# The first chunk of a scan with buffers of its own, a wider spread of its decays, and a first gate in halves, in a fused scan and feed-forward kernel

## The chip, the cores and the metric

The kernel runs on one core of a Trainium2 chip. The metric is the device time of one execution in microseconds (us). The engines are PE (matrix products), DVE (vector), ACT (scalar), POOL (GpSimd) and SP, which issues the DMAs.

## The reference

A chunked state-space scan over 4 batches, 8 heads and 768 positions (head width 32, state width 16) is followed by a gated feed-forward layer over the 3072 tokens (model width 256, hidden width 1536). All is fp32.

```python
# scan, chunk by chunk, for each batch and head
cum = np.cumsum(log(clip(a, 1e-6, 1)), axis=-1)
L = exp(cum[..., :, None] - cum[..., None, :]) * causal
y_intra = ((C @ B.T) * L) @ x
y_inter = (C @ state) * exp(cum)[..., None]
y = y_intra + y_inter
state = exp(sum(la)) * state + sum_j(B_j x_j exp(cum[-1] - cum_j))
# feed-forward over the tokens
gate = 1 / (1 + exp(-(x @ w_gate)))
out = (gate * (x @ w_val)) @ w_out
```

## The kernel before

The 768 positions are cut into six chunks of 128. A chunk has four units, one for each batch b. A unit transposes B and C (`pt`, copied to `bct` by ACT), multiplies them (`pcb`), builds decays (`ab`, a scan on DVE), multiplies products and decays (`m`, DVE) and adds decayed B (a second part of `m`, "bdec", on POOL in the first chunk), multiplies with x (`py`, `mm`) and carries a state (`st`, `sb`). The result y goes to SBUF as `xh` (from the second chunk on in two parts, `xh` and `xl`), one quarter of its columns from each unit.

The first chunk is treated apart (`FirstUnit`). It works on two halves of 64 positions, so a unit has two results: `py` and `mm`. The state between the halves goes through `tr`, a transpose on DVE, to four more matmuls into `mm` (line 642), with `cd`, which is C times decays (`pc`, `pp`). In its `spread`, PE copies decays of 32 rows (b, head) to all partitions: sixteen matmuls of 32x64 into `pa`, which DVE then scans to `ab`. `bct` and `m` have two buffers each, `pcb` has one. The transposed and copied halves of y are read in two steps: `early` for the first, the end of `result` for the second.

After a chunk's scan its feed-forward tokens follow: 12 gates `pg` and 12 values `pv` (f = 0 to 11), the product `h`, and four projections `po` over three blocks of four f each. In the first chunk weights are whole fp32 values (`wr`, prepared in "split" steps on ACT, DVE and POOL, lines 308 to 323) and a gate takes four PE instructions; later ones use two fp32r parts `w` (prepared in "part" steps on ACT and POOL, lines 334 and 336) and six matmuls. From the second chunk on POOL also makes the low part of `h` (line 736).

No scheduler of the compiler orders this: `run()` takes tasks, each with a due time (`DUES` or a formula of constants), and emits their steps in the order of a small plan of engine times. So one table sets the order on every engine. PSUM has three `mm` buffers (pt, pa, pc, mm, pg, pv, po), four banks for `pcb` and one for `py`. A matmul writes a buffer only when its readers are done with it.

Of the kernel before, what the change touches and what calls it, by code (L numbers as in the profile page):

```python
# [17 lines left out]
DUES = {  # L18
# [8 lines left out]
}  # L27
WARM = 3
# [12 lines left out]
GV0 = 1.75  # L41
GV0_T = 3.3
PART = 48.0
PROJ_T = 4.2
P0 = 37.3
UNIT0 = 3.4
CONV_D = 3.0
CONV = -23.4
UNIT1 = 61.1
UNIT1_D = 6.4  # L50
FFN1 = 107.3
UNIT_T = 3.4
UNIT_D = 0.0
AHEAD = 21.9
STATE = 14.7
SPARE = 4.0
# [7 lines left out]
def tile_ssd_then_gated_ffn(  # L64
# [68 lines left out]

    of_b = const.tile([NB * H, NB], F32, name="of_b")
    eye_bh = eye[: NB * H, : NB * H]
    nc.vector.tensor_reduce(of_b, eye_bh.rearrange("p (b h) -> p b h", b=NB), axis=mybir.AxisListType.X, op=ALU.add)
    head = const.tile([NB * H, H], F32, name="head")
    nc.vector.tensor_reduce(head, eye_bh.rearrange("p (b h) -> p h b", b=NB), axis=mybir.AxisListType.X, op=ALU.add)
    of_row = hp.tile([NB * H, P], F32, tag="h4", name="of_row")
# [212 lines left out]
    class Unit:  # L352
# [15 lines left out]
        def products(self):  # L368

            c, b, u = self.c, self.b, self.u  # L370
            needs = [("bc", u), ("bct", u - 1 if c > 1 else -1), ("cb", u - 2), ("cd", u - 2)] + ([("x", 0, NB - 1)] if c == 1 else [])
# [5 lines left out]
            yield step("act", 0.9 if c else 1.1, [("cb", u - 2), ("cd", u - 2)], [("bct", u)], banks=-1)  # L377
            self.bct = wk.tile([P, 4, L], F32, tag="bct", name=f"bct{self.nm}")
            if c:
                nc.scalar.copy(self.bct[:, :2].rearrange("p k l -> p (k l)"), pt[:, : 2 * L])  # L380
            else:
                nc.scalar.copy(self.bct[:, 0], pt[:, :L])
            for g in range(NG):
                nc.scalar.mul(self.bct[:, 2 + g], pt[:, L : 2 * L], of_g[:, g : g + 1])
            if c == 0:
                nc.scalar.copy(self.bct[:, 1, L2:], pt[:, L + L2 : 2 * L])
            units[u] = self
            if u <= NB:
                yield step("pe", 0.85 if c else 0.47, [], [("cb", u)], cb=1)
                self.multiply()  # L390
# [158 lines left out]
    class FirstUnit(Unit):  # L549
# [11 lines left out]
        def spread(self):  # L561

            b, u = self.b, self.u
            yield step("pe", 1.15, [("a0",)], banks=1)
            pa = ps_mm.tile([P, 512], F32, tag="mm", name=f"pa{b}")
            for k in range(H):
                h = b * H + k
                for i in range(2):
                    rows = slice(32 * i, 32 * i + 32)
                    one = eye[rows, 32 * i + h : 32 * i + h + 1].broadcast_to([32, L2])  # L570
                    nc.tensor.matmul(
                        pa[i * L2 : (i + 1) * L2, k * L2 : (k + 1) * L2], one, ac[rows, i * L2 : (i + 1) * L2],
                        start=True, stop=True,
                    )
            yield step("dve", 1.22, [], [("scan", u)], banks=-1)
# [6 lines left out]
        def multiply(self):  # L582
            self.pcb = ps_cb.tile([P, NQ, 512], F32, tag="pcb", name=f"pcb{self.nm}")
            for q in range(NQ):
                qs = slice(32 * q, 32 * q + 32)
                for i in range(2):
                    half = slice(i * L2, (i + 1) * L2)
                    nc.tensor.matmul(
                        self.pcb[half, q, : NG * L2], self.bct[qs, 0, half], self.bct[qs, 2:4, half],
                        start=True, stop=True,  # L590
                    )
# [21 lines left out]
        def result(self):  # L613
            u, b = self.u, self.b
            yield step("dve", 0.68, [("cb", u), ("scan", u), ("ph", u - 2)], [("mult", u)], cb=-1)
            nc.vector.tensor_tensor(
                out=self.second()[:, :, :L2].rearrange("p (q g) l -> p q g l", g=NG),
                in0=self.pcb[:, :, : NG * L2].rearrange("p q (g l) -> p q g l", g=NG),
                in1=self.dec.rearrange("p (q g) l -> p q g l", g=NG), op=ALU.mult,
# [88 lines left out]
    def gate(k, f):  # L708
        yield step("pe", GV_T / 2 if k else GV0, needs_of(k, f, 0), [("pg", k, f)] + used(k, f, 0), banks=1)
        pm = products_of(k, f, 0)  # L710
        yield step("act", ACT_MM, [], [("sig", k, f)], banks=-1, g=1)
        gs[k, f] = wk.tile([P, 512], F32, tag="g", name=f"g{k}_{f}", bufs=3)
        nc.scalar.activation(gs[k, f], pm, AF.Sigmoid)  # L713

    def value(k, f):
        makes = [("pv", k, f)] + ([("gv", k)] if f == NF - 1 else [])
        yield step("pe", GV_T / 2 if k else GV0, needs_of(k, f, 1) + [("pg", k, f)], makes + used(k, f, 1), banks=1)
        pm = products_of(k, f, 1)
        if k == 0:
# [21 lines left out]
    def needs_of(k, f, j):  # L741
        return [("w" if k else "whole", f // 2 * 2 + j)] + [("x", k, i) for i in range(NB)] + ([("pv", k, f - 1)] if f else [])

    def products_of(k, f, j):
# [87 lines left out]
    nc.vector.tensor_scalar(out=ac, in0=a0, scalar1=1e-6, scalar2=1.0, op0=ALU.max, op1=ALU.min)  # L832
    nc.vector.memset(ac.rearrange("p (s l) -> p s l", l=L2)[:, :, :1], 0.0)
    chunks = "p (c l) -> p c l"

# [152 lines left out]
```

## Time and profile before

| | |
|---|---|
| runs | 387.51, 387.96, 388.02 us, median 387.96 |
| profiled execution | 387.17 us, span 384.7 us, mean granted PE clock 0.972 |
| DVE, ACT, POOL busy | 203.0, 149.8, 166.6 us |
| moved by DMA | 31.39 MB, mean 82 GB/s |

A group's line gives source line, engine, operation, tiles (output and inputs), count, then busy time, mean ns and the idle time before it with what ended it. A timeline row gives start, length, engine, line, output and inputs, count and, in brackets, the idle time before it and its releaser. Two groups of the first chunk's feed-forward and two of POOL's:

```profile
L323 POOL TENSOR_TENSOR wr<-wr 128x512 int32<-128x512 int32 x18 | 21.8, 1218 | 35.6 <-ACT wr L321 31.3
L336 POOL TENSOR_TENSOR w<-wr,w 128x512 fp32r<-128x512 f32 x18 | 27.6, 1532 | 4.5 <-ACT w L334 4.4
```

### The profile page before, as it was taken

How to read it: one execution, taken by the hardware profiler on the slowest of the kernel's cores; microseconds unless marked ns; L12 is line 12 of the kernel's file. 1: busy time of each engine (PE TensorE's matmuls, PEld its weight loads, DVE VectorE, ACT ScalarE, POOL GpSimd, SP SyncE). 2: the span in 40 equal slices, each digit the busy share in tenths (PEclk: the TensorE clock that was granted, in tenths of full speed). 3: DMA queues.
4: the chain of work that ended last, by engine and by line, in shares of the span. 5: the costliest groups of instructions: out<-in, count | busy, mean ns of one | idle time of the engine just before them, and what ended most of it. 6: DMA issues, size and time to landing. Idle time of an engine off the chain costs nothing.

```text
span 384.7 us, 6190 instructions
## 1 busy us (share of the span) xinstructions
PE 375.2 (98%) x2368; PEld 287.8 (75%) x2368; DVE 203.0 (53%) x311; ACT 149.8 (39%) x319; POOL 166.6 (43%) x136
## 2 busy tenths in 40 slices
PE   8689999999999999999999999999999999999996
PEld 4444444677788888877888877888877888888885
DVE  4676779977893566457870157970155220122201
ACT  3364564533465521254340254340254340235310
POOL 2353345465889950334770034780032340044410
PEclk9658999999999999999999999999999999999999
DMA  7899793075530087138600038600000000000000
GB/s 87 237 369 386 102 212 88 1 146 129 84 108 2 10 123 185 41 42 152 157 9 27 27 36 158 159 8 29 27 9 0 2 0 29 27 0 2 0 24 32
DMA packets 107462, 31.39 MB, mean 82 GB/s; under 512 B 76554, under 2 KB 102730, under 8 KB 107434
## 3 DMA queue, kind: packets, MB, share of 16 engines
q1 hardware_dynamic: 107434, 31.01, 35.0%
q8 instruction: 19, 0.31, 0.3%
q14 instruction: 9, 0.07, 0.1%
HBM read 27.66 MB, written 3.34 MB: 81 GB/s over the span
## 4 chain that ended last, share of the span: by engine, by line
PE 93%; SPq 3%; DMA 1%; DVE 1%; issue 1%; POOL 0%; ACT 0%
PE pv L760 22%; PE pg L760 21%; PE po L793 14%; PE po L794 7%; PE pg L751 6%; PE po L783 6%; PE pv L751 5%; PE pcb L489 3%; PE py L527 2%; PE py L519 2%; SPq L253 1%; SPq L267 1%; DMA wr<-in_moe_w_val_dram 1%; PE pt L375 1%; PE po L790 1%; PE py L446 1%
## 5 line engine op out<-in xcount | busy, mean ns | idle before, releaser
L736 POOL TENSOR_TENSOR h<-g,h 128x512 fp32r<-128x512 f32 x60 | 92.1, 1537 | 129.7 <-ACT h L734 129.6
L760 PE MATMUL pg<-xh,w 128*128 128x512 f32 x240 | 85.4, 396 | 0.0
L760 PE MATMUL pv<-xh,w 128*128 128x512 f32 x240 | 84.6, 393 | 0.0
L793 PE MATMUL po<-w,h 128*128 128x512 f32 x228 | 81.0, 399 | 0.0
L730 DVE TENSOR_TENSOR g<-pv,g 128x512 f32<-128x512 f32 x60 | 41.2, 686 | 67.7 <-PE pv L760 59.3
L794 PE MATMUL po<-w,h 128*128 128x256 f32 x228 | 64.0, 281 | 0.0
L734 ACT CAST h<-g 128x512 fp32r<-128x512 f32 x60 | 37.2, 620 | 65.0 <-DVE g L730 64.7
L713 ACT ACTIVATE g<-pg 128x512 f32<-128x512 f32 x72 | 43.0, 597 | 45.9 <-PE pg L760 25.9
L760 PEld LDWEIGHTS pv<-xh,w 128*128 128x128 f32 x240 | 45.0, 188 | 10.7 <-issue 1.4
L760 PEld LDWEIGHTS pg<-xh,w 128*128 128x128 f32 x240 | 45.1, 188 | 10.0 <-ACT xh L538 0.3
L793 PEld LDWEIGHTS po<-w,h 128*128 128x128 f32 x228 | 42.8, 188 | 10.8 <-issue 0.2
L401 DVE TENSOR_TENSOR_SCAN ab<-ab,delta 128x1024 f32<-128x1024 f32 x20 | 49.2, 2461 | 2.5 <-DMA ab<-a_z 2.5
L760 PE MATMUL pg<-xl,w 128*128 128x512 f32 x120 | 46.8, 390 | 0.0
L760 PE MATMUL pv<-xl,w 128*128 128x512 f32 x120 | 46.8, 390 | 0.0
L794 PEld LDWEIGHTS po<-w,h 128*128 128x128 f32 x228 | 43.1, 189 | 0.3
L808 DVE TENSOR_TENSOR o<-po,o 128x256 f32<-128x256 f32 x20 | 8.5, 424 | 63.8 <-ACT o L806 63.8
L323 POOL TENSOR_TENSOR wr<-wr 128x512 int32<-128x512 int32 x18 | 21.8, 1218 | 35.6 <-ACT wr L321 31.3
L806 ACT COPY o<-po 128x256 f32<-128x256 f32 x20 | 7.4, 372 | 69.6 <-PE po L794 69.1
L336 POOL TENSOR_TENSOR w<-wr,w 128x512 fp32r<-128x512 f32 x18 | 27.6, 1532 | 4.5 <-ACT w L334 4.4
L477 POOL TENSOR_TENSOR sb<-st,of_h 128x256 f32<-128x256 f32 x20 | 18.7, 940 | 20.9 <-DVE st L469 17.5
L760 PEld LDWEIGHTS pv<-xl,w 128*128 128x128 f32 x120 | 22.5, 188 | 4.5
L760 PEld LDWEIGHTS pg<-xl,w 128*128 128x128 f32 x120 | 22.6, 188 | 4.1
(105 smaller groups left out, 436.4 us busy)
## 6 DMA issues: line engine op xcount, KB each, us to landing
ab<-a_z SPq DMA_DIRECT2D x20, 512.0 KB
wr<-in_moe_w_gate_dram SPq DMA_DIRECT2D x6, 512.0 KB
wr<-in_moe_w_val_dram SPq DMA_DIRECT2D x6, 512.0 KB
wr<-in_moe_w_out_dram SPq DMA_DIRECT2D x6, 512.0 KB
out_dram<-o SPq DMA_DIRECT2D x24, 128.0 KB
xn<-in_x_dram SPq DMA_DIRECT2D x10, 256.0 KB
bn<-in_B_dram SPq DMA_DIRECT2D x40, 32.0 KB
cn<-in_C_dram SPq DMA_DIRECT2D x40, 32.0 KB
```

The costliest lines, as they stand in the source:

```text
L323: nc.gpsimd.tensor_tensor(out=lw.bitcast(I32), in0=hw.bitcast(I32), in1=lw.bitcast(I32), op=ALU.add)
L336: engines[eng].tensor_tensor(out=lo, in0=lw, in1=hi.bitcast(F32), op=ALU.subtract)
L401: nc.vector.tensor_tensor_scan(out=t.rearrange("p h l -> p (h l)"), data0=t.rearrange("p h l -> p (h l)"), data1=delta.rearrange("p h l -> ...
L713: nc.scalar.activation(gs[k, f], pm, AF.Sigmoid)
L730: nc.vector.tensor_tensor(out=g, in0=pm, in1=g, op=ALU.mult)
L734: copies[eng](hh, g)
L736: engines[eng].tensor_tensor(out=hl, in0=g, in1=hh.bitcast(F32), op=ALU.subtract)
L751: nc.tensor.matmul(pm, whole[f // 2 * 2 + j][:, kt, fs], xb[0][0][:, kt], start=(kt == 0), stop=(kt == NK - 1))
L760: nc.tensor.matmul(pm, w[:, part, kt, fs], xx[:, kt], start=(i == 0), stop=(i == 3 * NK - 1))
L783: nc.tensor.matmul(acc[:, :DM], hs[k, f][:, js], whole[NF + f // 2][:, f % 2], start=(f == 0), stop=(f == NF - 1))
L793: nc.tensor.matmul(acc, hh, w.rearrange("p i m -> p (i m)"), start=(f == 0), stop=False, skip_group_check=True)
L794: nc.tensor.matmul(acc[:, :DM], hl, w[:, 0, :], start=False, stop=(f == NF - 1), skip_group_check=True)
```

## The change

Four things are changed.

1. The spread uses two matmuls a unit, over 32 rows and 512 columns each. Their input `apart` (the decays times a table of heads) is made once, half by DVE and half by POOL; `of_b` and `head` become tables of 64 rows.
2. In the first chunk `bct` lies in buffers of its own for all four units, taken from tiles that `h` uses later, and the four products `pcb` lie in one PSUM tile, made as soon as `bct` is there.
3. The first gate and the first value are computed in halves of 256 columns: the first halves need x of batches 0 and 1 only.
4. `DUES` and the constants beside it are others, so the order moves on every engine.

```diff
 DUES = {
-    "spread0": 133, "products0_0": -376, "result0_0": -282, "before1_0": -70, "products1_0": 182, "decays1_0": 10,
+    "p": 51.5, "before0_0": 75.7, "state0_0": 85.1, "x1_0": 142.5, "before1_0": -134.0, "decays1_0": -57.3,
...
-GV0_T = 3.3
-PART = 48.0
+GV0_T = 3.4
+PART = 41.9
...
-P0 = 37.3
-UNIT0 = 3.4
-CONV_D = 3.0
-CONV = -23.4
-UNIT1 = 61.1
-UNIT1_D = 6.4
-FFN1 = 107.3
-UNIT_T = 3.4
+P0 = 35.5
+UNIT0 = 4.5
+CONV_D = 6.3
+CONV = -30.0
+UNIT1 = 60.6
+UNIT1_D = 8.2
+FFN1 = 85.9
+UNIT_T = 14.9
...
-AHEAD = 21.9
-STATE = 14.7
+AHEAD = 46.7
+STATE = 30.0
...
-        free = {"sp": 1.0, "pe": 1.2 + 1.7 * WARM, "act": 3.5, "dve": 4.8, "pool": 4.2, "none": 0.0}
+        free = {"sp": 1.0, "pe": 1.2 + 1.7 * WARM, "act": 3.5, "dve": 6.0, "pool": 6.2, "none": 0.0}
...
-            self.bct = wk.tile([P, 4, L], F32, tag="bct", name=f"bct{self.nm}")
+            if c:
+                self.bct = wk.tile([P, 4, L], F32, tag="bct", name=f"bct{self.nm}")
+            else:
+
+                if ("bct", b // 2) not in got:
+                    got["bct", b // 2] = hp.tile([P, 2, 4, L], F32, tag=f"h{b // 2}", name=f"bct{self.nm}")
+                self.bct = got["bct", b // 2][:, b % 2]
...
-            if u <= NB:
-                yield step("pe", 0.85 if c else 0.47, [], [("cb", u)], cb=1)
+            if c == 0:
+                yield step("pe", 0.47, [], [("cb", u)])
+                self.multiply()
+            elif u == NB:
+                yield step("pe", 0.85, [("mult", v) for v in range(NB)], [("cb", u)], cb=1)
                 self.multiply()
...
-            for k in range(H):
-                h = b * H + k
-                for i in range(2):
-                    rows = slice(32 * i, 32 * i + 32)
-                    one = eye[rows, 32 * i + h : 32 * i + h + 1].broadcast_to([32, L2])
-                    nc.tensor.matmul(
-                        pa[i * L2 : (i + 1) * L2, k * L2 : (k + 1) * L2], one, ac[rows, i * L2 : (i + 1) * L2],
-                        start=True, stop=True,
-                    )
+            for i in range(2):
+                rows = slice(32 * i, 32 * i + 32)
+                nc.tensor.matmul(
+                    pa[i * L2 : (i + 1) * L2], of_b2[rows, b : b + 1].broadcast_to([32, L2]),
+                    apart[rows].rearrange("p h l -> p (h l)"), start=True, stop=True,
+                )
...
-            self.pcb = ps_cb.tile([P, NQ, 512], F32, tag="pcb", name=f"pcb{self.nm}")
+
+            if "pcb" not in got:
+                got["pcb"] = ps_cb.tile([P, NQ, NB, NG * L2], F32, tag="pcb", name="pcb0")
+            self.pcb = got["pcb"][:, :, self.b]
...
+        if (k, f) == (0, 0):
+
+            yield step("pe", GV0 / 2, [("whole", 0), ("x", 0, 0), ("x", 0, 1)], [("pg half",)], banks=1)
+            pm = first_half(0)
+            yield step("pe", GV0 / 2, [("x", 0, 2), ("x", 0, 3)], [("pg", k, f)])
+            second_half(0, pm)
...
+    def half_of(j, pm, columns):
+        for kt in range(NK):
+            nc.tensor.matmul(
+                pm[:, columns], whole[j][:, kt, :P], xb[0][0][:, kt, columns], start=(kt == 0), stop=(kt == NK - 1)
+            )
...
+    apart = hp.tile([R2, H, L2], F32, tag="h2", name="apart")
+    for i, engine in ((0, nc.vector), (1, nc.gpsimd)):
+        rows = slice(32 * i, 32 * i + 32)
+        engine.tensor_tensor(
+            out=apart[rows], in0=ac[rows, i * L2 : (i + 1) * L2].rearrange("p (o l) -> p o l", o=1).broadcast_to([32, H, L2]),
+            in1=head2[rows].rearrange("p (h o) -> p h o", o=1).broadcast_to([32, H, L2]), op=ALU.mult,
+        )
```

On PE, the end of the first chunk's scan before the first gate. A row is a line, an operation, the output and inputs with their numbers, and a shape; the first number behind a name is the unit's or the f's. Before:

```order
L642 MATMUL mm_1_379<-cd_1_334,tr_1_406 32x2x64 x4
L630 MATMUL py_2_429<-m_2_332,xn_1_144 32x80
L598 MATMUL pc_3_456<-bct_3_367,perm 128x64
L630 MATMUL py_3_466<-m_3_447,xn_1_144 32x80
L642 MATMUL mm_2_430<-cd_2_421,tr_2_459 32x2x64 x4
L642 MATMUL mm_3_467<-cd_3_461,tr_3_493 32x2x64 x4
L751 MATMUL pg_0_509<-xh_353,wr_148 128x512 x2
L751 MATMUL pv_0_532<-xh_353,wr_199 128x512 x2
```

In the changed kernel the same place reads (the rows of py alternate with rows of mm in both; one of each group is shown):

```order
L647 MATMUL py_2_366<-m_2_297,xn_1_145 32x80
L659 MATMUL mm_1_327<-cd_1_283,tr_1_355 32x2x64 x4
L615 MATMUL pc_3_394<-bct_2_217,perm 128x64
L659 MATMUL mm_2_367<-cd_2_359,tr_2_399 32x2x64 x4
L647 MATMUL py_3_417<-m_3_353,xn_1_145 32x80
L784 MATMUL pg_0_442<-xh_309,wr_147 128x256 x2
L659 MATMUL mm_3_418<-cd_3_402,tr_3_446 32x2x64 x4
L784 MATMUL pv_0_458<-xh_309,wr_173 128x256 x2
```

The third unit's mm stands ahead of the fourth unit's py, and the fourth unit's mm stands between the first half of the gate and that of the value.

On DVE, the first chunk's products and transposes in the changed kernel, from the fourth decay scan on (`wt` and `wr` are the weight split):

```order
L633 TENSOR_TENSOR m_2_297<-pcb_175,ab_2_212 128x8x64
L655 STREAM_TRANSPOSE tr_0_295<-mm_0_265 128x32
L633 TENSOR_TENSOR m_1_222<-pcb_175,ab_1_200 128x8x64
L315 TENSOR_SCALAR wt_313<-wt_313 128x512
L679 SCALAR_TENSOR_TENSOR st_110<-tr_0_295,pp_184 128x32
L317 TENSOR_SCALAR wt_313<-wt_313 128x512
L633 TENSOR_TENSOR m_3_353<-pcb_175,ab_3_227 128x8x64
L655 STREAM_TRANSPOSE tr_1_355<-py_1_326 128x32
L618 TENSOR_TENSOR cd_2_359<-pc_2_322,pp_184 128x128
L655 STREAM_TRANSPOSE tr_1_355<-mm_1_327 128x32
L315 TENSOR_SCALAR wt_350<-wt_350 128x512
L322 SCALAR_TENSOR_TENSOR wr_173<-wr_173,wt_313 128x512
```

The third unit's product goes ahead of the second's, and operations of the weight split lie between the second unit's transposes and the third's.

On POOL, the end of chunk 1's gates before (`w` are weight parts, `h` the low parts of h, `sb` the state's matrix for the scan):

```order
L736 TENSOR_TENSOR h_9_1335<-g_9_1321,h_9_1335 128x512
L336 TENSOR_TENSOR w_1358<-wr_512,w_1358 128x2x256
L736 TENSOR_TENSOR h_10_1384<-g_10_1345,h_10_1384 128x512
L477 TENSOR_TENSOR sb_114<-st_110,of_h 128x256
L477 TENSOR_TENSOR sb_115<-st_111,of_h 128x256
L736 TENSOR_TENSOR h_11_1467<-g_11_1439,h_11_1467 128x512
```

And in the changed kernel:

```order
L341 TENSOR_TENSOR w_1305<-wr_439,w_1305 128x2x256
L494 TENSOR_TENSOR sb_116<-st_112,of_h 128x256
L341 TENSOR_TENSOR w_1355<-wr_455,w_1355 128x2x256
L766 TENSOR_TENSOR h_10_1371<-g_10_1339,h_10_1371 128x512
L494 TENSOR_TENSOR sb_114<-st_110,of_h 128x256
L766 TENSOR_TENSOR h_11_1412<-g_11_1367,h_11_1412 128x512
L494 TENSOR_TENSOR sb_115<-st_111,of_h 128x256
L341 TENSOR_TENSOR w_1385<-wr_474,w_1385 128x2x256
```

The last weight part stands behind the last h of the chunk, and ten parts instead of eight come between the first h and the last operation that this projection needs.

More of the change, by code (lines that the diff above doesn't have):

```diff
@@ L132, in tile_ssd_then_gated_ffn @@
     nc.gpsimd.tensor_copy(delta2, eye2.rearrange("p (o l) -> p o l", o=1).broadcast_to([P, H, L2]))
[L134 to L138, printed above, removed]
+    R2 = 2 * NB * H
+    of_b2 = const.tile([R2, NB], F32, name="of_b")
+    eye_bh = eye[:R2, :R2]
+    nc.vector.tensor_reduce(
+        of_b2, eye_bh.rearrange("p (o b h) -> p b o h", o=2, b=NB), axis=mybir.AxisListType.XY, op=ALU.add
+    )
+    head2 = const.tile([R2, H], F32, name="head")
+    nc.vector.tensor_reduce(head2, eye_bh.rearrange("p (k h) -> p h k", h=H), axis=mybir.AxisListType.X, op=ALU.add)
+    of_b, head = of_b2[: NB * H], head2[: NB * H]
     of_row = hp.tile([NB * H, P], F32, tag="h4", name="of_row")
@@ L588, in multiply @@
                     nc.tensor.matmul(
-                        self.pcb[half, q, : NG * L2], self.bct[qs, 0, half], self.bct[qs, 2:4, half],
+                        self.pcb[half, q], self.bct[qs, 0, half], self.bct[qs, 2:4, half],
                         start=True, stop=True,
@@ L716, in value @@
         makes = [("pv", k, f)] + ([("gv", k)] if f == NF - 1 else [])
-        yield step("pe", GV_T / 2 if k else GV0, needs_of(k, f, 1) + [("pg", k, f)], makes + used(k, f, 1), banks=1)
-        pm = products_of(k, f, 1)
+        if (k, f) == (0, 0):
+            yield step("pe", GV0 / 2, [("whole", 1), ("pg half",)], banks=1)
+            pm = first_half(1)
+            yield step("pe", GV0 / 2, [("pg", k, f)], makes)
+            second_half(1, pm)
+        else:
+            yield step("pe", GV_T / 2 if k else GV0, needs_of(k, f, 1) + [("pg", k, f)], makes + used(k, f, 1), banks=1)
+            pm = products_of(k, f, 1)
         if k == 0:
@@ L742, in needs_of, with first_half, second_half @@
         return [("w" if k else "whole", f // 2 * 2 + j)] + [("x", k, i) for i in range(NB)] + ([("pv", k, f - 1)] if f else [])
+    def first_half(j):
+        pm = ps_mm.tile([P, 512], F32, tag="mm", name=f"p{'gv'[j]}0_0")
+        half_of(j, pm, slice(0, 2 * P))
+        return pm
+    def second_half(j, pm):
+        half_of(j, pm, slice(2 * P, 4 * P))
+    def half_of(j, pm, columns):
[3 more added lines that the diff above has]
+            )
     def products_of(k, f, j):
```

19 lines of the change are left out of this document (12 added, 7 removed), and 14 rows, old and new, of the table DUES.

## The prediction

> **What bounds the kernel now.** I read the busy times and the chain that ended last first.
>
> ```profile
> PE 375.2 (98%) x2368; PEld 287.8 (75%) x2368; DVE 203.0 (53%) x311; ACT 149.8 (39%) x319; POOL 166.6 (43%) x136
> PE 93%; SPq 3%; DMA 1%; DVE 1%; issue 1%; POOL 0%; ACT 0%
> ```
>
> PE works for 98% of the span and carries 93% of the chain. The list of what PE waited for comes next; behind each name stand the sum of the waits, their number and the longest.
>
> ```profile
> PE mm L642 <- DVE tr L638: 2.4, 1, 2.4
> PE mm L630 <- issue: 0.5, 1, 0.5
> ```
>
> These and shorter ones belong to the first chunk's scan. The PE timeline says when it is over (start, length, line, output and inputs, count, idle time before):
>
> ```profile
> 13.84 0.73 PE L588 MATMUL pcb<-bct 32*64 32x128 f32 x16 [1.15 <-DVE m L616]
> 14.51 0.34 PE L630 MATMUL py<-m,xn 64*32 64x80 f32 x1
> 14.96 0.34 PE L630 MATMUL mm<-m,xn 64*32 64x80 f32 x1
> 26.30 1.16 PE L642 MATMUL mm<-cd,tr 32*32 32x128 f32 x16
> 27.89 3.75 PE L751 MATMUL pg<-xh,wr 128*128 128x512 f32 x4 [0.43 <-issue]
> 33.53 1.88 PE L751 MATMUL pg<-xh,wr 128*128 128x512 f32 x4
> 379.93 1.58 PE L801 MATMUL po<-w,h 128*128 128x256 f32 x12
> ```
>
> From the first gate at 27.89 to the last matmul, which ends at 381.51, the list names no wait of PE. So the time can change in three ways only: that start moves, work moves across it, or a new wait appears in the dense stretch. The last rows but one also show the clock: a gate takes 3.75 us at the start and 1.88 us later. The windows give the granted clock (length, busy times of PE, PEld, DVE, ACT, POOL, then clock, DMA share, GB/s):
>
> ```profile
> 11.00:12.00 1.00, 1.00 (x24) 0.85 (x19) 1.00 (x2) 0.00 (x0) 1.00 (x1) 0.85 1.35 233
> 12.00:28.00 16.00, 11.09 (x220) 6.12 (x219) 11.91 (x32) 7.88 (x24) 5.92 (x9) 0.50 0.94 305
> 32.00:33.00 1.00, 1.00 (x3) 0.39 (x2) 0.00 (x0) 1.00 (x3) 0.09 (x1) 0.91 1.02 373
> ```
>
> A mean of 0.85 puts the drop to half at 11.70, a mean of 0.91 puts the release at 32.18. The dense work of the first 4.29 us runs at half rate, which loses 2.15 us.
>
> **The spread.** Before, sixteen small matmuls a unit spread the decays; now two wide ones do, after DVE and POOL have made their input.
>
> ```profile
> 9.53 2.08 PE L571 MATMUL pa<-ac,eye 32*64 32x64 f32 x64 [0.29 <-DVE ab L577]
> 4.71 0.60 POOL L682 TENSOR_TENSOR apb<-ap,of_b 32x256 f32<-32x256 f32 x1 [0.40 <-DVE ap L677]
> 7.14 2.34 DVE L577 TENSOR_TENSOR_SCAN ab<-pa,delta 128x512 f32<-128x512 f32 x2 [2.51 <-PE pa L571]
> 13.10 0.69 DVE L616 TENSOR_TENSOR m<-pcb,ab 128x512 f32<-128x512 f32 x1
> ```
>
> A unit cost PE 2.08/2 = 1.04 us. A 512-column instruction at full rate takes 1.88/4 = 0.47 us; two matmuls are four of them, so 1.9 us if they follow one another and 0.95 us if the two halves, which lie in other rows and columns, overlap. I take 1.0, beside the value before (32 instructions a unit there fit into 1.04 us as well). The new products cost 0.69 us on DVE (the length of an m of as many elements) and 0.60 x 2 = 1.2 us on POOL at most. The first scan therefore starts near 7.1, as before, and the four scans of 1.17 us with one m between end by about 12.5. That ends far ahead of the first py, so both ends of this cost, 0 and +3.5 us on PE, are hidden by the arrival of C, next.
>
> **The chain to the first gate.** In the new order py_0 stands behind the transposes of the last B and C. Their landing has no row; the nearest is the weight tile:
>
> ```profile
> 7.77 0.58 SPq L293 DMA_DIRECT2D wr<-in_moe_w_gate_dram  x1
> 8.91 1.03 SPq L253 DMA_DIRECT2D cn<-in_C_dram  x1
> 12.21 0.66 ACT L308 ACTIVATE wt<-wr 128x512 f32<-128x512 f32 x1 [1.66 <-DMA wr<-in_moe_w_gate_dram]
> 15.53 0.41 POOL L608 TENSOR_TENSOR m<-bn,ab 128x128 f32<-128x128 f32 x1 [1.97 <-PE mm L630]
> 20.38 0.69 DVE L616 TENSOR_TENSOR m<-pcb,ab 128x512 f32<-128x512 f32 x1
> 18.76 0.41 DVE L312 TENSOR_SCALAR wt<-wt 128x512 uint32<-128x512 uint32 x1
> 19.09 1.29 DVE L317 SCALAR_TENSOR_TENSOR wr<-wr,wt 128x512 uint32<-128x512 uint32 x2
> 21.85 0.20 DVE L638 STREAM_TRANSPOSE tr<-py 128x32 f32<-128x32 f32 x1
> 24.22 0.29 DVE L601 TENSOR_TENSOR cd<-pc,pp 128x128 f32<-128x128 f32 x1
> 20.99 0.93 DVE L662 SCALAR_TENSOR_TENSOR st<-tr,pp 128x32 f32<-128x32 f32 x1
> 22.08 0.27 ACT L650 COPY xh<-py 128x128 f32<-128x128 f32 x1 [0.69 <-DVE tr L638]
> ```
>
> The weight tile was issued by 8.35 and used at 12.21, 3.9 us later; C was issued by 9.94, so it is there near 13.8. Transposes and one pc take 0.8 us at half clock: py_0 at 14.6. Own buffers do not free the next steps. The array m still has two buffers, so the third decay on POOL waits for py_0 as it did at 15.53: it ends at 16.0, and m_2 0.69 later. The four products now share one tile, and PE's fourth set stands behind m_2, m_1 behind the fourth set: 0.73 us and a hand-over (0.9 in all), then 0.69, so py_1 starts at 18.4. It takes 0.8 us (the first and last of the 32 rows at 14.51 and 14.96); m_3 (0.69), a transpose (0.2) and the xh copy (0.27) stand before py_2, at 20.5. Its transposes stand on DVE behind three operations of the weight split (0.41, 0.65 and 0.41, the middle one up to 1.0 if it is held up like the st at 20.99) and a cd (0.29): ready at 22.6. Then mm_2 (1.16/2 = 0.58), py_3 (0.8): 24.1. The chain of before holds an unexplained wait for issue of 0.5 us; half of one brings the first half gate to 24.3. Ends: 22.8 if the shared tile and the split cost nothing, 26.3 if every step is as late as before, when the last mm ran at 26.30. The start moves by 27.89 - 24.3 = **-3.6 us**.
>
> **What moves behind that start.** The fourth mm now stands between the half gate and the half value: 0.58 us, and 0.3 us until its transposes are there (two of 0.2 on DVE, one hidden). **+0.9 us**; ends 0.6 and 1.6. Halves have the columns of the whole, so they cost nothing more; a half gate at half clock is 1.88 us. The first value needs its weights whole; before, that tile came out of POOL at
>
> ```profile
> 17.60 0.66 ACT L308 ACTIVATE wt<-wr 128x512 f32<-128x512 f32 x1 [4.73 <-DMA wr<-in_moe_w_val_dram]
> 23.01 1.04 POOL L323 TENSOR_TENSOR wr<-wr 128x512 int32<-128x512 int32 x1 [0.77 <-ACT wr L321]
> ```
>
> 24.05, and it has until about 27, so its cost is nothing.
>
> **The clock.** From 11.70 to 32.18 are 20.48 us, six times 3.413. If the release comes only at such points, it can come at 28.77 when dense work begins before 25.36. From 24.3 to 28.77 the half clock then loses 2.2 us, and the term is **+0.05 us**. If it stays at 32.18, 7.9 us run at half, 3.9 are lost, and the term is +1.8. Before, the stretch 25.36 to 28.77 held 0.9 us of the gate and no release followed; now 2.5 of its 3.4 us would be dense, the rest the fourth mm and its wait. I take the early release, at two to three against one. The Trainium skill, "TensorE: Matmul & The Clock Gate", Part 1, says that half rate is the default and that a busy window of about 3.4 us, which runs freely and does not start with the kernel, releases it. By that rule the release falls on such a point, the trace's six equal stretches agree, and a start moved by less than a window may win nothing: that is the second rival below.
>
> **The dense stretch.** The order of the weight parts on POOL moves: of those needed by the projection of chunk 1, more are left when its first h comes. These rows are that stretch before (PE's first gate of chunk 1 at 103.39 follows the last po):
>
> ```profile
> 101.31 2.08 PE L783 MATMUL po<-wr,h 128*128 128x256 f32 x8
> 102.32 2.47 POOL L477 TENSOR_TENSOR sb<-st,of_h 128x256 f32<-128x256 f32 x1 [0.20 <-DVE st L469]
> 107.87 2.76 POOL L736 TENSOR_TENSOR h<-g,h 128x512 fp32r<-128x512 f32 x1 [1.81 <-ACT h L734]
> 113.13 3.29 POOL L336 TENSOR_TENSOR w<-wr,w 128x512 fp32r<-128x512 f32 x1
> 125.19 3.29 POOL L736 TENSOR_TENSOR h<-g,h 128x512 fp32r<-128x512 f32 x1
> 136.03 1.27 POOL L736 TENSOR_TENSOR h<-g,h 128x512 fp32r<-128x512 f32 x1
> 140.95 1.20 POOL L477 TENSOR_TENSOR sb<-st,of_h 128x256 f32<-128x256 f32 x2 [3.65 <-DVE st L469]
> 107.25 2.28 DVE L401 TENSOR_TENSOR_SCAN ab<-ab,delta 128x1024 f32<-128x1024 f32 x1
> 139.71 0.39 PE L793 MATMUL po<-w,h 128*128 128x512 f32 x1
> ```
>
> POOL ran 11 h and 8 w without a gap from 107.87 to 137.30, 29.4 us, and then had 3.65 us to spare. Three of these took 2.76, 3.29 and 3.29 instead of about 1.3: a scan ran on DVE at those times (107.25 is the first), 1.8 us each. Now there are 12 h, 10 w and 3 sb up to the last w, with five scans among them: 22 x 1.26 + 3 x 0.6 + 5 x 1.84 = 38.7 us. The first h comes 4.5 us after the chunk's first gate, X, so the last w is ready at X + 43.2. PE wants it at the third block of the first projection, after four blocks of eight matmuls (0.355 us a pair, 5.7 us in all): 139.71 + 5.7 - 103.39 = X + 42.0. **+1.2 us** of waiting on PE; ends 0 (scans that miss POOL's work) and 4 (a late first h on top). No other place in the later chunks loses cover: POOL is 43% busy over the whole span, and no PE wait is listed there now.
>
> **Sum.** -3.6 + 0.9 + 0.05 + 1.2 = -1.45 us. The profiled execution took 387.17 us, its span 384.7; the sum gives 385.7. The median of the runs, 387.96, is 0.79 above that execution, so 386.5 there. A measurement tells about 0.2% here, 0.78 us.
>
> **Rivals.**
> - *The release stays at 32.18*: the fourth mm and its wait break the window. Against it: most of the window is dense. 386.5 + 1.8 = 388.3: no change. Chance 0.16.
> - *The chain hardly shortens*: shared tile, two buffers of m and the split on DVE hold it, and the gate starts at 26. The row at 20.99, a state update of 128x32 elements that took 0.93 us where an m of sixteen times as many takes 0.69, speaks for it. 386.5 + 1.7 = 388.2: no change. 0.10.
> - *POOL's last weight part ends the other way*: the two w and three sb more wait for long scans and for a first h that comes two to three microseconds late, as the sb at 102.32 took 2.47 us where two at 140.95 took 1.20. The wait at the projection grows from 1.2 to about 4.2: 389.5, slower. It decides when that w ends later than X + 45.5. 0.13.
> - *No wait at the projection, and the 0.5 us wait for issue falls away*: POOL has room, as its 3.65 us to spare show. 386.5 - 1.7 = 384.8, faster. 0.13.
>
> **How the numbers follow.** My forecast has 0.48, with a range of its own from 385.6 to 387.2. Faster: 0.48 + 0.13, less 0.01 for its upper edge, 0.60. Same: 0.16 + 0.10 and that edge, 0.27. Slower: 0.13. The range for 8 in 10 runs from the last rival's 384.8 to just above the first two, 388.6.
>
> **What would show it.** Right: the first half gate at 24.3, a clock of 1.00 from 28.8, one wait of PE of about a microsecond at the first projection of chunk 1, released by POOL's w, and no other wait behind the gate. Wrong: a clock of 0.50 up to 32, a gate after 25.4, a POOL wait of 3 us, or a PE wait for h or x in a later chunk, which I have priced at nothing.

## The result and the profile after

The changed kernel takes 385.42 us (384.88 to 385.97), the kernel before 387.83 us (387.51 to 388.02): the ratio on record is 0.9941 (the two medians alone give 0.9938), with a 95% interval from 0.9924 to 0.9957. That is faster by 2.4 us, 0.6%; the forecast was 386.5, faster by 1.45. Its profiled execution took 384.88 us, 2.29 us less than that of before, with a span of 382.5.

The busy line and the list of what PE waited for, after:

```profile
PE 373.1 (98%) x2264; PEld 286.0 (75%) x2264; DVE 205.9 (54%) x312; ACT 151.2 (40%) x319; POOL 163.3 (43%) x137
PE py L647 <- POOL m L625: 1.5, 1, 1.5
PE pcb L605 <- DVE tr L655: 1.0, 1, 1.0
PE pt L383 <- DVE h L758: 0.9, 1, 0.9
PE mm L659 <- DVE tr L655: 0.5, 1, 0.5
```

The first wait of this list lies at py_2, the third unit's py. The list puts it down to POOL's m, but that m (20.42 to 20.83) is the fourth unit's, which py_2 does not read. What py_2 needs is the one PSUM buffer of py, and the last reader of py_1 is ACT's copy to `xh`, which ends at 20.82:

```profile
20.55 0.27 ACT L667 COPY xh<-py 128x128 f32<-128x128 f32 x1 [0.95 <-DVE tr L655]
20.91 0.31 PE L647 MATMUL py<-m,xn 64*32 64x80 f32 x1 [1.47 <-POOL m L625]
```

In all eleven profiles of the changed code with the new order, py_2 starts 0.09 to 0.11 us behind the end of that copy, whatever the list names. So the copy is what it waits for, as far as the rows can tell; no experiment below changes this buffer.

PE's timeline where the first chunk's scan ends, after (line 784 is the half gate and half value), and its last row:

```profile
15.10 0.72 PE L605 MATMUL pcb<-bct 32*64 32x128 f32 x16
16.80 0.73 PE L605 MATMUL pcb<-bct 32*64 32x128 f32 x16 [0.97 <-DVE tr L655]
23.41 0.65 PE L659 MATMUL mm<-cd,tr 32*32 32x128 f32 x8 [0.51 <-DVE tr L655]
24.70 2.07 PE L784 MATMUL pg<-xh,wr 128*128 128x256 f32 x4
26.70 0.65 PE L659 MATMUL mm<-cd,tr 32*32 32x128 f32 x8
27.29 1.89 PE L784 MATMUL pv<-xh,wr 128*128 128x256 f32 x4
58.37 0.33 PE L383 MATMUL pt<-eye,bn 128*128 128x128 f32 x1 [0.85 <-DVE h L758]
377.71 1.58 PE L845 MATMUL po<-w,h 128*128 128x256 f32 x12
```

And the windows with the granted clock, third value from the end:

```profile
12.00:28.00 16.00, 12.19 (x226) 7.21 (x225) 13.29 (x33) 8.85 (x25) 7.14 (x8) 0.60 0.99 320
28.00:29.00 1.00, 1.00 (x4) 0.81 (x3) 0.59 (x2) 1.00 (x2) 0.00 (x0) 0.58 1.04 377
29.00:32.00 3.00, 3.00 (x12) 2.16 (x11) 1.13 (x4) 0.86 (x2) 1.04 (x1) 1.00 1.05 388
```

The gate starts at 24.70 instead of 27.89, and 0.59 us of mm lie behind that start, so dense work begins, in effect, at 25.29. The clock runs at half from 15.2 (3.2 of the 16 us after 12 are at full rate) to 28.84: 13.64 us, four times 3.41, where it was six times before. The last matmul ends at 379.29 instead of 381.51.

These numbers make a sum that holds for every kernel in this study but the two with the wrong order. Let S be the start of dense work (the first gate, plus the mm that lies behind it), R the release of the clock, W the waits of PE behind S. What is left of PE's end after S, W and (R - S)/2 is the dense work itself, all in us (R is worked out from the mean clock of the window in which it changes, as in the prediction, and is good to a few hundredths; the experiments that give the other rows follow below):

| kernel, its profiled execution | S | R | W | PE's end | dense work |
|---|---|---|---|---|---|
| before | 27.89 | 32.18 | 0 | 381.51 | 351.5 |
| changed | 25.29 | 28.84 | 0.85 | 379.29 | 351.4 |
| changed, second execution | 25.65 | 28.36 | 1.57 | 380.14 | 351.6 |
| whole_first_gate | 25.26 | 29.04 | 1.57 | 380.19 | 351.5 |
| old_spread | 25.24 | 26.80 | 1.55 | 379.31 | 351.7 |
| one_product_buffer | 26.78 | 30.62 | 0 | 379.98 | 351.3 |
| early_third_m | 24.17 | 27.36 | 0.47 | 377.80 | 351.6 |
| no_scan_ahead_of_h | 24.86 | 27.76 | 0 | 377.77 | 351.5 |
| last_part_twice | 25.45 | 28.04 | 2.1 | 380.49 | 351.6 |
| last_part_earlier | 24.86 | 29.32 | 0.3 | 378.84 | 351.5 |
| third_m_and_two_moves | 24.05 | 28.02 | 0.2 | 377.58 | 351.3 |
| and_split_held_back | 25.57 | 28.87 | 0 | 378.53 | 351.3 |

Dense work is 351.3 to 351.7 us in all of them. So PE's end is read from three numbers: S, R - S and W. Of these R - S is not the kernel's own: it lies between 1.6 and 4.5 us, with no order by kernel, and the half-rate stretch is in each of these profiles a whole number of 3.41 us (two to six), at another place each time. Half of it ranges over 1.45 us. S scatters as well: the five profiles whose program is the changed one up to the gate (changed twice, no_scan_ahead_of_h, last_part_twice, last_part_earlier) have 24.86 to 25.65.

From PE's end to the measured time there are 5.5 to 5.7 us in ten of these rows, but 6.1 and 6.2 in early_third_m and third_m_and_two_moves. In every run of those two kernels the time exceeds the profile's span by 2.9 to 3.0 us, in the runs of all others here by 1.9 to 2.6. No run shows why, and the medians of two kernels can differ by half a microsecond for this reason alone.

### The profile page after: what moved, and what is told of

Same layout as the page of the kernel before. It is cut to its first block, busy times and chain, and to the rows that moved or that the text cites. A ratio compares the mean times of both kernels' runs of the same rounds, so it can differ in the third digit from the quotient of the medians.

```text
span 382.5 us, 5978 instructions
## 1 busy us (share of the span) xinstructions
PE 373.1 (98%) x2264; PEld 286.0 (75%) x2264; DVE 205.9 (54%) x312; ACT 151.2 (40%) x319; POOL 163.3 (43%) x137
## 4 chain that ended last, share of the span: by engine, by line
PE 84%; SPq 8%; DMA 6%; issue 1%; DVE 0%; DVEq 0%
PE pv L804 22%; PE pg L804 22%; PE po L837 14%; PE po L838 7%; PE po L827 6%; PE pcb L506 3%; DMA wr<-in_moe_w_gate_dram 3%; SPq L264 2%; SPq L302 2%; PE py L544 2%; PE py L536 2%; PE pv L795 2%; DMA a<-in_a_dram 2%; SPq L258 1%; PE pg L795 1%; SPq L272 1%
## 5 line engine op out<-in xcount | busy, mean ns | idle before, releaser
L766 POOL TENSOR_TENSOR h<-g,h 128x512 fp32r<-128x512 f32 x60 | 89.6, 1493 | 124.0 <-ACT h L764 123.9
L418 DVE TENSOR_TENSOR_SCAN ab<-ab,delta 128x1024 f32<-128x1024 f32 x20 | 50.9, 2551 | 6.2 <-DMA ab<-a_z 6.1
L341 POOL TENSOR_TENSOR w<-wr,w 128x512 fp32r<-128x512 f32 x18 | 28.8, 1602 | 8.8 <-ACT w L339 6.3
L494 POOL TENSOR_TENSOR sb<-st,of_h 128x256 f32<-128x256 f32 x20 | 14.8, 740 | 31.1 <-DVE st L486 21.1
L804 PEld LDWEIGHTS pv<-xl,w 128*128 128x128 f32 x120 | 22.6, 188 | 4.4
L804 PEld LDWEIGHTS pg<-xl,w 128*128 128x128 f32 x120 | 22.6, 188 | 4.1
```

The lines of the kernel that those rows point to most:

```text
L341: engines[eng].tensor_tensor(out=lo, in0=lw, in1=hi.bitcast(F32), op=ALU.subtract)
L418: nc.vector.tensor_tensor_scan(out=t.rearrange("p h l -> p (h l)"), data0=t.rearrange("p h l -> p (h l)"), data1=delta.rearrange("p h l -> ...
L494: engines[eng].tensor_tensor(out=sb[b], in0=st[b].rearrange("p (o r d) -> p o r d", o=1, r=1).broadcast_to([P, NG, NQ, D]), in1=of_h.rearr ...
L766: engines[eng].tensor_tensor(out=hl, in0=g, in1=hh.bitcast(F32), op=ALU.subtract)
L804: nc.tensor.matmul(pm, w[:, part, kt, fs], xx[:, kt], start=(i == 0), stop=(i == 3 * NK - 1))
```

## The experiments

The theory after the first comparison: the earlier start pays one for one; the chain to it is held by the shared product tile, by the buffers of m and by DVE's queue; waits behind it decide the rest. Rivals: the halves, the wide spread (through the clock), the new order alone. In the sessions of these experiments the kernel before had medians of 387.67 to 387.82 us, so they can be compared.

**The halves.** Whole gate and value, all else in order:

```diff
             yield step("pe", GV0 / 2, [("whole", 0), ("x", 0, 0), ("x", 0, 1)], [("pg half",)], banks=1)
-            pm = first_half(0)
             yield step("pe", GV0 / 2, [("x", 0, 2), ("x", 0, 3)], [("pg", k, f)])
+            pm = first_half(0)
             second_half(0, pm)
```

> The changed kernel, but its first gate and first value are computed whole again; the order of all other work is the same. Theory (the gain is the earlier start of dense work, and the clock is released at the end of a window of 3.41 us that was mostly dense): the gate starts after the fourth unit's mm and its xh copy, near 26.7 instead of 24.70, while the mm of 0.6 us no longer lies behind it: +1.4 us of start. The window 25.4 to 28.84 is then only 60% dense; if the release slips to 32.2 the time is about 388.2, if it stays at 28.84 about 386.1. I take the slip. Rival (the halves are worth nothing, since the gate waits elsewhere): 385.4, as the changed kernel.

Measured: 386.18 us, ratio 0.9957 (0.9936 to 0.9979). Its PE timeline:

```profile
22.41 0.65 PE L659 MATMUL mm<-cd,tr 32*32 32x128 f32 x8 [0.51 <-DVE tr L655]
24.68 0.65 PE L659 MATMUL mm<-cd,tr 32*32 32x128 f32 x8 [0.91 <-DVE tr L655]
25.26 3.78 PE L784 MATMUL pg<-xh,wr 128*128 128x256 f32 x8
```

The expected start of 26.7 and the slip of the release were both missed: in this execution the clock stayed full up to 18.8, and the third mm came at 22.41 instead of 23.41. Counted from that mm, S is 2.85 us later here and 1.88 us later with halves (23.41 to 25.29; 1.87 or 1.88 in seven other profiles with halves), so the halves are worth 1.0 us of start. The times agree with that only roughly (386.18 against 385.42 and 385.67 for the changed kernel), since waits fall differently; see below. That 386.18 is near the 386.1 expected without a slip is luck: the start is 1.4 us earlier than expected there, and a wait of 1.57 us at the projection, which the expectation did not have, about makes up for it.

**The spread.** The sixteen narrow matmuls a unit instead of the two wide ones, without `apart`:

```diff
-            for i in range(2):
...
-                    apart[rows].rearrange("p h l -> p (h l)"), start=True, stop=True,
+            for k in range(H):
...
+                        pa[i * L2 : (i + 1) * L2, k * L2 : (k + 1) * L2], one, ac[rows, i * L2 : (i + 1) * L2],
```

> The changed kernel with the sixteen narrow matmuls a unit of before for the spread; the product apart and its two instructions are gone, the order of all other work is the same. Theory: the clock drops to half at 11.7 us again instead of 15.2, some small products of the first chunk take half as long again, the first half gate moves by 0.3 us at most, since C's landing and the products hold it: 385.4 to 385.9. Rival (the wide spread brings the gain, by the clock or by earlier scans): 386.5 or more.

Measured: 384.45 us, ratio 0.9910 (0.9889 to 0.9930). The half gate starts at 24.89 (24.70 with the wide ones), so the spread is hidden, as its cost was in the prediction. The drop of the clock came at 16.56, not at 11.7: the narrow matmuls do not bring the drop forward, and the place of the drop is not the spread's. The rival falls, and the expected 385.4 to 385.9 was missed as well. Whether the wide spread costs something (the median is about 1 us lower without it) stays open, since clock and waits of these few executions differ by as much.

**The product buffers.** One PSUM buffer for the four products, as before:

```diff
-            if "pcb" not in got:
-                got["pcb"] = ps_cb.tile([P, NQ, NB, NG * L2], F32, tag="pcb", name="pcb0")
-            self.pcb = got["pcb"][:, :, self.b]
+            self.pcb = ps_cb.tile([P, NQ, 512], F32, tag="pcb", name=f"pcb{self.nm}")
```

> The changed kernel with one PSUM buffer for the four products, as before, and the same order. Theory (the shared tile already makes the fourth set of products wait for the third m, so own buffers free little): the second set now waits for the third m and the fourth for the second m; py_1 moves from 18.66 to about 19.6, the half gate by 1.0 us: 386.2 to 386.6. Rival A (own buffers bring all the gain): 387.5 or more. Rival B (they bring nothing): 385.4.

Measured: 385.38 us, ratio 0.9935 (0.9913 to 0.9957). The PE timeline:

```profile
18.29 0.73 PE L602 MATMUL pcb<-bct 32*64 32x128 f32 x16 [0.89 <-DVE m L630]
26.20 2.07 PE L781 MATMUL pg<-xh,wr 128*128 128x256 f32 x4
```

The fourth set of products comes at 18.29 instead of 16.80, and the half gate at 26.20 instead of 24.70: 1.5 us, more than the 1.0 expected, and the waits are the expected ones. S of 26.78 is 1.1 to 1.9 us later than in the five profiles named above. The median does not show it; it is that of rival B, and only the rows speak against that rival. This execution has no wait at all behind the start where the changed kernel has 0.85 or 1.57; that the other executions lack it too would explain the median, but is not shown. The buffers of `bct`, changed together with these, were not tested by themselves.

**The third m.** A buffer of its own (the space of `apart`), and its two operations made ahead of the first `cd`:

```diff
+                pool, tag = (hp, "h2") if self.b == 2 else (wk, "m")
-                self.m = wk.tile([P, H, L2 + N], F32, tag="m", name=f"m{self.nm}")
+                self.m = pool.tile([P, H, L2 + N], F32, tag=tag, name=f"m{self.nm}")
...
+            if b == 0:
+                units[2].decayed("pool")
+                units[2].multiplied()
             self.cd = wk.tile([P, NG, L2], F32, tag="cd", name=f"cd{self.nm}")
```

> The changed kernel, where the third unit's m has a buffer of its own and its product is made ahead of the first cd on DVE, and so ahead of the second set of products on PE; the rest of the order is the same. Theory (PE's wait of 0.97 us before the fourth set of products comes from the third m's buffer and place): that wait goes, m_1 starts 1.0 us earlier, and DVE's next operation, the weight split, holds part of it back: half gate earlier by 0.4 to 0.7 us, 384.7 to 385.1. Rival (DVE's queue takes all of it back): 385.4.

Measured: 383.87 us, ratio 0.9905 (0.9882 to 0.9928). PE now runs the second and fourth set of products in one go, and the half gate starts 1.1 us earlier:

```profile
15.73 0.69 PE L606 MATMUL pcb<-bct 32*64 32x128 f32 x32
23.59 2.07 PE L797 MATMUL pg<-xh,wr 128*128 128x256 f32 x4
```

So the shared tile did hold the chain, through the third m: the list had put PE's wait of 0.97 us down to a transpose, but here the fourth set of products is over at 16.42, before that transpose begins at 16.55. The gain in start is somewhat more than the 0.4 to 0.7 expected. It is not the clock's, which stayed full up to 20.5 here: with the same edit in third_m_and_two_moves, below, the clock fell at 14.4 and the half gate still starts at 23.47.

**The changed kernel once more.**

> The changed kernel once more, as the measure for the others of this group. Theory (dense work takes 351.4 us whatever the kernel; the end is its start plus that, plus the waits behind it, plus half the time from the start to the release of the clock, which falls on a grid of 3.41 us whose place differs from execution to execution): runs scattered over about 1.7 us, median 385.0 to 386.0, the start of the half gate at 24.7, and a release at another place than 28.84.

Measured: 385.67 us, ratio 0.9937 (0.9911 to 0.9963), runs from 383.30 to 386.73, twice the expected scatter; the half gate starts at 25.07. This profile shows what the first did not. In the first profile, DVE, POOL and PE stand like this at two places:

```profile
54.55 1.04 POOL L328 TENSOR_TENSOR wr<-wr 128x512 int32<-128x512 int32 x1 [1.61 <-ACT wr L326]
54.67 3.07 DVE L418 TENSOR_TENSOR_SCAN ab<-ab,delta 128x1024 f32<-128x1024 f32 x1 [0.84 <-DMA ab<-a_z]
57.66 0.66 DVE L758 TENSOR_TENSOR h<-pv,g 128x512 f32<-128x512 f32 x1
141.82 1.30 POOL L341 TENSOR_TENSOR w<-wr,w 128x512 fp32r<-128x512 f32 x1
142.38 2.89 DVE L418 TENSOR_TENSOR_SCAN ab<-ab,delta 128x1024 f32<-128x1024 f32 x1 [2.95 <-DMA ab<-a_z]
```

And in the second execution of the same kernel:

```profile
53.68 2.28 DVE L418 TENSOR_TENSOR_SCAN ab<-ab,delta 128x1024 f32<-128x1024 f32 x1
54.50 2.29 POOL L328 TENSOR_TENSOR wr<-wr 128x512 int32<-128x512 int32 x1 [1.63 <-ACT wr L326]
55.88 0.66 DVE L758 TENSOR_TENSOR h<-pv,g 128x512 f32<-128x512 f32 x1
141.20 2.55 DVE L418 TENSOR_TENSOR_SCAN ab<-ab,delta 128x1024 f32<-128x1024 f32 x1 [2.01 <-DMA ab<-a_z]
141.56 3.27 POOL L341 TENSOR_TENSOR w<-wr,w 128x512 fp32r<-128x512 f32 x1
144.89 0.51 PE L837 MATMUL po<-w,h 128*128 128x512 f32 x1 [1.57 <-POOL w L341]
```

In each of these pairs the operation that begins first takes its time alone or little more (1.04, 1.30, 2.28, 2.55 us), and the other is lengthened by nearly the time that the two overlap (0.79 of 0.92 us, 0.61 of 0.74, 1.25 of 1.46, 1.97 of 2.19). So a scan and a POOL operation exclude each other, and the one that begins first wins. In the first execution POOL began 0.12 us ahead of the scan at 54.6: scan and h are late, and PE waits 0.85 us at pt. In the second the scan began first, PE has no wait there and comes to the projection 1 us earlier; there the last weight part meets the next scan, begins 0.36 us behind it, takes 3.27 instead of 1.30 us, and PE waits 1.57 us. The Trainium skill, "SBUF — State Buffer", section "Who interferes with whom", says that issue order decides who blocks; these rows agree.

**The first of these waits.** The scan emitted behind the h of f = 7:

```diff
+            if u == NB:
+                late.append(scan)
+            else:
+                scan()
...
+            if f == 7:
+                late.pop()()
```

> The changed kernel with one pair on DVE exchanged: the first decay scan of chunk 1 stands behind the h of f = 7 instead of ahead of it. Theory: PE's wait of 0.85 us at pt near 58 goes, and chunk 1 begins 0.85 us earlier. Then the last weight part on POOL comes as late as a scan on DVE near 141 and takes 3.3 us where the scan begins first, and PE waits about 1.6 us for it: runs in two groups, 384.2 to 384.8 and 385.8 to 386.4. Rival (that wait at pt simply goes, POOL has time): 384.5.

Measured: 384.00 us, ratio 0.9910 (0.9879 to 0.9941), runs from 382.48 to 386.02. The profile shows no wait of PE behind the start, neither at pt nor at the projection. There the last part begins at 140.17 and the scan at 140.34, 0.17 us behind it. That the other wait comes up in its place where the scan is first, as I expected, would fit the runs at 385 and 386, but no profile of this kernel shows it. The two groups that I expected do not appear: one run lies in each, and the median is nearer to the rival's 384.5.

**The second.** First the last weight part is made twice, then it is moved:

```diff
+        for _ in range(2 if i == NW - 1 else 1):
-        engines[eng].tensor_tensor(out=lo, in0=lw, in1=hi.bitcast(F32), op=ALU.subtract)
+            engines[eng].tensor_tensor(out=lo, in0=lw, in1=hi.bitcast(F32), op=ALU.subtract)
```

> The changed kernel with the last weight part on POOL made twice (the second writes the same values). Theory (that part is ready 1.2 us before the projection of chunk 1 needs it, and a scan on DVE then stands between): its second copy meets the scan, takes about 3.3 us and ends near 146.4, so PE waits about 2.1 us: 387.0 to 388.0. Rival A (an instruction of 1.3 us alone): a wait of 0.1 to 0.3 us, 385.5 to 385.8. Rival B (POOL has room for it): 385.4.

Measured: 386.38 us, ratio 0.9974 (0.9955 to 0.9992). POOL's row (both copies) and PE's wait:

```profile
140.61 4.54 POOL L342 TENSOR_TENSOR w<-wr,w 128x512 fp32r<-128x512 f32 x2
PE po L838 <- POOL w L342: 2.1, 1, 2.1
```

The wait is the 2.1 us expected; the median is 0.6 us under the expected range. The expectation set the whole wait on top of the changed kernel's time, but that kernel has waits of 0.85 and 1.57 us in its own two profiles; against the second of these, PE's end here is only 0.35 us later.

```diff
+            last_part.append(lambda: nc.gpsimd.tensor_tensor(out=lo, in0=lw, in1=hi.bitcast(F32), op=ALU.subtract))
...
+        if (k, f) == (1, 10):
+            last_part.pop()()
```

> The changed kernel with the last weight part on POOL put behind the h of f = 10 instead of behind the h of f = 11 and two sb; nothing else moves. Theory (in some executions a DVE scan starts just ahead of that part, which then takes 3.3 us and holds PE for 1.6): the part is done near 139.5, no execution waits for it, and only the wait of up to 0.85 us at pt stays: 383.3 to 385.3, median 384.5. Rival (that wait is rare or hidden): median 385.5, as the changed kernel.

Measured: 383.73 us, ratio 0.9894 (0.9879 to 0.9909), runs from 382.79 to 384.43.

```profile
138.31 1.31 POOL L341 TENSOR_TENSOR w<-wr,w 128x512 fp32r<-128x512 f32 x1
PE py L541 <- ACT g L742: 0.3, 1, 0.3
```

The part ends at 139.62 and nobody waits for it. The median is 1.7 to 1.9 us below those of the changed kernel, more than the 0.9 expected; the largest such wait in a profile is 1.57, so part of the difference is where the start, the clock and the wait at pt fell (S is 24.86 in this profile).

**The order alone, and the code alone.** The code before with the table and constants of the changed kernel, and the reverse (the diff is the first and the constants of the one shown with the change):

> The kernel before with the table and constants of the changed one; spread, buffers and gate as before. Theory (the earlier start needs the products and the buffers together with an order for them): the dense start moves by less than half of what the change moves it, 386.6 to 388.6, waits as the trace shows them. Rival (the order is the change): 385.0 to 385.9.

> The changed code with the table and constants of before. Theory (table and code are fitted to each other): waits of several microseconds appear, 388 or more. Rival (the buffers and the halves bring the gain, whatever the order): 385.0 to 386.0.

Measured: 404.47 us, ratio 1.0433 (1.0410 to 1.0457), and 403.52 us, ratio 1.0400 (1.0377 to 1.0424). One row of each, of the order alone and of the code with the old order:

```profile
44.33 0.45 PE L375 MATMUL pt<-eye,bn 128*128 128x128 f32 x1 [13.74 <-DMA bn<-in_B_dram]
```

```profile
63.63 3.78 PE L795 MATMUL pv<-xh,wr 128*128 128x512 f32 x4 [7.58 <-POOL wr L328]
```

The first kernel's gate starts at 26.81, 1.1 us earlier than before, and then loses 13.74 us to a load of B for the next chunk. SP issues that load from 39.98 on, no later than in the changed kernel (40.06); but PE asks for it right behind its first gate, at 30.6, where the changed kernel has its first such transpose at 54.77. So it is PE's order that does not fit. The second one's half gate starts at 22.74, earlier than in any other kernel here, and loses 7.58 us to a weight tile. My expectation for the first was right on the start (less than half of the change's 3.2 us) and wrong by far on the time (386.6 to 388.6). Neither half can be used as it stands without the other; what a table fitted to the old code would give, these two runs do not show.

**What the runs point to.** The third m early, the scan behind h and the last part earlier, together; then also the split of three weight tiles held back on DVE until the third unit's transposes.

> Three edits together: the third m early with a buffer of its own, the h of f = 7 ahead of the scan, the last weight part earlier. Theory, by the sum (dense start 24.2, dense work 351.4, no wait behind it, 1.6 for the clock, 3.2 for the tail, 2.5 around the span): 382.9, runs from 382.0 to 383.8. Rival (the edits take from each other): 383.9, as the third m alone.

> The same three edits, and the weight split of the second to fourth tiles held back on DVE until the third unit's transposes are done. Theory (DVE's queue is what holds the chain after the shared tile): py_2 and its transposes come about 1.2 us earlier, the half gate near 22.4: 381.3 to 382.3. Rival (the first value then waits for its weights, or POOL holds the fourth m): 382.9 or more.

Measured: 383.55 us, ratio 0.9891 (0.9878 to 0.9904), runs from 383.45 to 383.75; and 384.44 us, ratio 0.9915 (0.9900 to 0.9930). The first is faster than both kernels of this case, 0.65 us above the sum's 382.9. In its profile (383.75) R - S is 3.97 us where I had set 3.2, which adds 0.4; a wait of 0.2 stands behind the start, and the time outside the span is 2.95 where I had set 2.5. By the medians it is hardly faster than the third m (383.87), the scan (384.00) or the last part (383.73) each by itself, and nearer to the rival's 383.9; by the medians of the spans it is 380.6 against 380.95, 381.65 and 381.35. So in good part the edits do take from each other. The second is worse and misses its 381.3 to 382.3: ACT's timeline shows why.

```profile
23.56 0.66 ACT L322 ACTIVATE wt<-wr 128x512 f32<-128x512 f32 x1 [2.80 <-DVE wr L333]
24.13 0.65 ACT L337 ACTIVATE wr<-wr 128x512 int32<-128x512 uint32 x1
24.69 0.41 ACT L701 COPY xh<-mm 128x128 f32<-128x128 f32 x2
```

The second and third unit's mm copies stand on ACT behind an operation that waits 2.8 us for the split that I held back, and the half gate starts at 24.99 after a wait of 1.75 us for them. The moved queue took back more than DVE gave. Nor did py_2 come 1.2 us earlier: it starts at 19.38 instead of 19.68, because ACT's copy of py_1 now ends at 19.28, behind a weight cast and a split, although its transpose on DVE was done at 17.81. The rival's time came true, neither of its two reasons did.

## Why the prediction was right, and where not

- *What bounds the kernel*: right. In all kernels but the two with the wrong order PE ends within 0.2 us of S + 351.5 + W + (R - S)/2.
- *The spread hidden, 0 on the path*: right; 24.89 against 24.70 for the half gate.
- *The chain to the gate, -3.6*: nearly right, -3.2 (24.70 instead of 24.3). The steps came at 15.40 (third decay, 15.6 predicted), 16.80 (fourth products), 18.66 (py_1, 18.4), 20.91 (py_2, 20.5) and 23.41 (third mm, 22.6 and what follows). One reading was wrong: the third m waited for the second set of products in the shared tile (15.10 to 15.82), not only for the decay; that it still began at 15.96, as the predicted 16.0 said, is luck. One wait was not in it: the third unit's last transpose stands behind a cd that waited 0.34 us for PE's pc, and was done at 23.36. Of the 2.6 us by which S moved, the rows put 1.0 down to the halves and 1.1 to 1.9 to the products' buffers; each was taken away alone, so the two need not add up, and `bct` and the order have no share of their own.
- *What moves behind the start, +0.9*: +0.59. The fourth mm waited for nothing.
- *The clock, +0.05*: (R - S)/2 is 1.78 instead of 2.15, so -0.37 in these two profiles. The term was mis-sized although the release came at 28.84, beside the predicted 28.77: I let the half clock cost from the half gate at 24.3 on, also through the 0.9 us of mm and wait that are a term of their own. From S, 25.2 by the same forecast, to 28.77 it costs 1.8 us, and the term would have been -0.36. The place of the release was luck: I took the points 11.70, 28.77 and 32.18 of one execution as fixed, and they keep their distance, not their place; the second execution has 28.36, the variants 26.80 to 30.62. So the rival that the release stays at 32.18 had no fixed point to stay at. The mm in the window did not prevent the release. The start does matter, against a grid that moves: in the table's profiles the release is the first point of that execution's grid at least 1.9 us behind the first gate, while a point 1.6 us behind it was passed over once (last_part_earlier) and taken once (code_with_old_order).
- *The wait at the projection, +1.2*: in the first profile 0, in the second 1.57, for the very operation named, the last weight part. The sum had the last part ready at X + 43.2, with five scans among POOL's work, and wanted at X + 42.0 (X is chunk 1's first gate). In the first execution only four scans met that work, the part was ready at X + 42.0 and wanted at X + 43.0; in the second the fifth scan met the last part itself, which was ready at X + 44.7 and wanted at X + 43.15. So a sum of POOL's operations cannot price it alone: what counts is which of two instructions begins first.
- *No other place loses cover*: wrong by 0.85 us at pt in the first profile, by the same kind of meeting of scan and POOL.

Summed for the first profile: -3.19 + 0.59 - 0.37 + 0.85 = -2.12, against 2.22 us between the two last matmuls; the forecast's -1.45 lies 0.7 above. Term by term the difference is +0.4 in the chain, -0.3 in the mm, -0.4 in the clock and -0.35 in the waits, where one of 0.85 at another place stands for the 1.2 foreseen. The direction and the start were foreseen; that the waits nearly cancel is luck. The measured 385.42 is 0.2 us below the forecast's own range of 385.6 to 387.2 and inside the wide one.

## What to carry to other kernels

Where one engine is busy to the end, write its end as start, fixed work, waits and clock, and check the fixed work across kernels first; then a difference of a microsecond can be put to one term. A median of a few executions cannot tell terms of less than about a microsecond when two engines exclude each other and a clock is released on a grid of its own; two profiles of the same kernel show which term moved. A wait's releaser in the list is the last one by the profile; check that it makes something the waiting instruction needs. An order table belongs to the code that it was made for: neither alone says what the other is worth.

## What the runs showed of the hardware

- In the table's profiles the clock's half-rate stretch was about 20.5, 13.65, 10.24 or 6.8 us long, whole numbers of 3.41 us, and began anywhere between 11.7 and 20.5 us of the span. The Trainium skill, "TensorE: Matmul & The Clock Gate", Part 1, has the window of 3.413 us that runs freely, and the trace agrees. It gives ±500 ns for the place of the transition; here the time from dense start to release lay between 1.6 and 4.5 us.
- A scan of 128x1024 takes 2.28 us alone, 2.89 or 3.07 when a POOL operation began 0.56 or 0.12 us ahead of it; a weight part of 128x512 on POOL takes 1.30 alone and 3.27 when it begins 0.36 us behind a scan. That order decides over 1.57 us on the critical engine.
